# Two transformer layers on one core: 160 planned stretches, lent buffers, a second shift on GpSimd and a lock

## The chip, the cores and the metric

The kernel runs on one core of one Trainium2 chip. The metric is the device time of one execution in microseconds (us), as the median over runs. Five engines work side by side, each on its own list of instructions: TensorE (PE in the profile, its weight loads PEld), VectorE (DVE), ScalarE (ACT), GpSimd (POOL) and SyncE (SP), which issues the transfers.

## The reference

Two layers with shared weights, each attention and then a dense block, over 2048 rows of width 512, 32 heads of width 16, 1792 hidden units, all bfloat16:

```python
def _A_ref(x, wqkv, wo):                       # H = 32, Dh = 16
    qkv = (x @ wqkv).reshape(B, S, 3, H, Dh).transpose(2, 0, 3, 1, 4)
    q, k, v = qkv[0], qkv[1], qkv[2]
    scores = jnp.einsum("bhqd,bhkd->bhqk", q, k) * (Dh ** -0.5)
    o = jnp.einsum("bhqk,bhkd->bhqd", softmax(scores), v)
    return o.transpose(0, 2, 1, 3).reshape(B, S, D) @ wo
def _B_ref(x, w1, b1, w2, b2):
    return gelu(x @ w1 + b1) @ w2 + b2         # tanh form
x = A_x
x = x + _A_ref(layernorm(x), A_wqkv, A_wo)
x = x + _B_ref(layernorm(x), B_w1, B_b1, B_w2, B_b2)
# and both lines once more
```

The exponentials of the softmax are the bulk of the work outside TensorE: 2 layers x 32 heads x 2048 x 2048.

## The kernel before

The work is cut into cells. A cell is the scores of one 128-row tile of keys for 512 columns of padded queries (`QP`, in which a mask on GpSimd, L1192, leaves one of two heads). There are 4096 cells: one matmul each at L1244, on a quarter of the array's rows, so up to four run together. Their results lie in banks of the accumulator memory `ps`; two slots of three banks are filled in turn.

A cell's exponential is taken in one of two ways. ScalarE (L1601) reads a slot of two or three cells and writes `pt`; or VectorE makes it from the bits of a 16-bit integer. That second way has a chain, `dchain`, on a pair of cells in a buffer `du` of four parts: VectorE converts each cell into part 0 (`dfirst`, L1396), GpSimd adds a constant into part 1 (`one`, L1473), and VectorE adds twice that constant to parts 0 and 1, giving 2 and 3 (`two`, L1478). The four parts are then each multiplied with a differently weighted copy of V (`VC`, L1175), so that a VectorE cell needs four matmuls with values where a ScalarE cell needs one. These value products (L1665) run in rounds of four on quarters of the array's columns; a quarter with nothing to do gets a matmul with zeros (L1673).

Only five of the sixteen key tiles of a layer may be VectorE cells (`KD`). Projections, output product and dense block (L556) are the rest of TensorE's work, and fillers (L1232) are matmuls without use, put where TensorE would otherwise stand still too long. GELU runs on ScalarE (L997), which must load another table before and after it.

No order is written out by hand. A planner, run while the program is built, holds a clock for each engine, a list of threads (scores, exponentials, values, projections, layer norms and so on) with priorities, pools of buffers, and a cost for each operation. It always takes the operation that can start first, and writes each engine's instructions in that order, with semaphore waits from the buffers read and written. Constants such as `OPENING`, `TAIL`, `SLACK`, `ALONE`, `PTURG` and `DUURG` steer it. What matters here is that an engine executes its list strictly in the order the planner gave it. Two of its rules are:

```python
        if op.eng == "pool":                   # in _ready: GpSimd behind a VectorE shift
            at = max(t, self.clock["pool"])
            for a, b in self.port_ops[-4:]:
                if a <= at < b - HEAD:
                    at = t = b - HEAD
```

```python
            if self.lend == 2 or s.clock["act"] < s.clock["pe"] + ALONE:   # in chance: a lone VectorE cell
                return self.ended
```

Exponentials use 15 units of `pt`, and at times units lent from memory that is not in use then: two parts of `K` of layer 1, `Q`, and a part of V. `du` has five buffers of its own and one lent late from `K` of layer 0. V of layer 1 shares its memory with partial sums of layer 0 (`PART`); its column of ones is set by one memset when those are done.

Of the kernel before, what the change touches and what calls it, by code (L numbers as in the profile page):

```python
# [13 lines left out]
H = 32  # L14
# [41 lines left out]
QUEUE = 4  # L56
RUSH = 4
# [128 lines left out]
class _Op:  # L186
    __slots__ = ("eng", "cost", "fns", "reads", "writes", "sem", "by", "tail", "prio", "mode", "slack", "late", "back", "port", "limit", "after")

    def __init__(self, eng, cost, fns, reads=(), writes=(), sem=None, by=1, tail=0.0, prio=None, mode="F", slack=None):
# [4 lines left out]
        self.limit = 1e9  # L194
        self.late, self.after = None, []
# [21 lines left out]
class _Sched:  # L217
# [76 lines left out]
    def _ready(self, op):  # L294
# [67 lines left out]
    def run(self):  # L362
        while True:
# [64 lines left out]
            if e == "dve" and op.port:  # L428
                self.port_ops.append((start, start + cost))
# [9 lines left out]
def bass_interleave_layers__mha_block__dense_activation_gelu__prompt_kernel(  # L439
# [15 lines left out]
    with ExitStack() as es:  # L455
# [22 lines left out]
        T["PT"].append(vf[0][:, 0:8192].rearrange("p (n q) -> p n q", q=512))  # L478
# [8 lines left out]
        T["DU"].append(late.rearrange("p (i j q) -> p i j q", i=4, j=2))  # L487
        T["VC"] = sb([128, NKD, 3, H * 17], BF16, "vc")
# [57 lines left out]
class _Plan:  # L546
# [12 lines left out]
    def init(self):  # L559
        T, hbm = self.T, self.hbm  # L560

        def load(dst, src, sem, keys, cost):
# [17 lines left out]
        yield ("need", ("otn", 0, (0, 0, 512), 3))  # L580
        yield _Op("pool", 1.0, lambda e: e.memset(T["V"][1][:, :, :, 16:17], 1.0),
                  writes=["V11"] + ["PART.0.%d" % g for g in range(8)])
        yield ("give", "v1ones")
# [100 lines left out]
    def ln_tile(self, c, t, dst, dkeys, quick):  # L684
# [7 lines left out]
        if not quick:  # L692
            yield _Op("sp", 0.3, lambda e: e.dma_start(dst(t), T["XLN"][:, x, :], transpose=True),
                      reads=["XLN.%d" % x], writes=dkeys(t), sem="dtr%d" % x, by=16, tail=3.5)
            yield ("rel", "xln", x)
            yield ("give", ("lnt", t, ph))
            return
# [14 lines left out]
    def proj(self, l, kind, i, c, src, skeys, ph, done):  # L712
# [44 lines left out]
        if kind == "K":  # L757
            keys = ["K%d.%d.%d" % (l, i, c)]
            if l == 1:
                keys += ["XL.%d" % t for t in range(4 * c, 4 * c + 4)]  # L760
                if c in LEND:
                    yield ("need", ("k1", c))
# [6 lines left out]
        else:  # L769
            yield _Op("dve", DV, lambda e: e.tensor_copy(T["V"][l][:, i, :, 0:16], pb.rearrange("p (h d) -> p h d", h=H)),  # L770
# [166 lines left out]
    def wlate(self, todo):  # L937
        over = ["K0.%d.%d" % (i, c) for i in (0, 1) for c in range(self.NQ)] + ["PART1.%d" % g for g in range(4)]
# [107 lines left out]
    def post(self, l, seg):  # L1046
# [20 lines left out]
        if prev:  # L1067
            yield ("need", ("gfree",) + prev)
        for p in range(NFC // 2):
# [69 lines left out]
    def setup_attention(self):  # L1139
        self.pas = self.passes()  # L1140
        self.alist, self.dlist, self.left, self.pvleft = [], [], [], {}
        self.base, self.span = {}, {}
        n = 0
        for pi, (l, seg, g, kts, part, final) in enumerate(self.pas):
            self.alist.append([(pi, kt, a) for kt in kts if kt not in KD[l] for a in range(4)])
            self.dlist.append([(pi, kt, a) for kt in kts if kt in KD[l] for a in range(4)])
            self.left.append(4 * len(kts))
            n += 4 * len(kts)
# [3 lines left out]
        self.total, self.scored, self.nd, self.pa, self.pv = n, 0, 0, 0, 0  # L1152
        for l in range(NL):
# [4 lines left out]
        self.cap = [2] * (DU // 2) + [1] * (DU % 2) + [2]  # L1158
# [8 lines left out]
    def vcopies(self):  # L1167
        T = self.T
        for l in range(NL):
            yield ("cond", lambda l=l: self.pv >= self.lead[l])  # L1170
            for j, kt in enumerate(KD[l]):
                yield ("need", ("V", l, kt, kt // 4))
                src = T["V"][l][:, kt, :, :].rearrange("p h c -> p (h c)")
                for i, w in enumerate(VW):
                    yield _Op("pool", 0.68, lambda e, j=j, i=i, w=w, src=src: e.tensor_scalar(  # L1175
                        T["VC"][:, j, i, :], src, w, 1.0, op0=ALU.mult, op1=ALU.mult),
                        reads=["V%d.%d" % (l, kt), "V%d1" % l], writes=["VC.%d.%d" % (j, i)])
# [99 lines left out]
    def take(self, c, free):  # L1277
        self.scored += 1
        self.left[c[0]] -= 1
        if self.left[c[0]] == 0:  # L1280
            free.append(self.s.tokens[("qp", c[0])])

    def join(self, op, d, b, extra, free):
# [15 lines left out]
        self.take(d, free)  # L1299
        self.nd += 1  # L1300

    def swap(self, op, start, cells, extra, free, sl):
        if extra or self.lend == 2 or len(cells) < 3 or not (self.open or self.s.pools["du"]):
            return
        if self.s.clock["dve"] > start + SWAP:
            return
# [3 lines left out]
        d = self.next_d({x[2] for x in cells[:-1]}, start)  # L1310
# [8 lines left out]
        if self.left[c[0]] == 1:  # L1319
            free.remove(self.s.tokens[("qp", c[0])])  # L1320
        self.pa = min(self.pa, c[0])
        self.alist[c[0]].insert(0, c)
        self.join(op, d, self.slots[sl][2], extra, free)

    def attach(self, op, start, cells, extra, free):
# [4 lines left out]
        for home in ("dbank", "misc"):  # L1330
            for b in list(pools[home]):
                if len(used) == 4 or self.lend == 2 or not (self.open or pools["du"]):
# [11 lines left out]
                self.join(op, d, b, extra, free)  # L1344

    def scores(self):
        u = 0
        pools = self.s.pools
        while True:
            sl = yield ("acq", "s")  # L1350
            cells = []
            for _ in self.slots[sl]:
# [7 lines left out]
            fns, reads, writes, free, extra = [], [], [], [], []  # L1360
            for c, b in work:
# [7 lines left out]
                self.take(c, free)  # L1369
            ahead = 0.065 + 0.4267 * self.held[1 - sl]  # L1370
            op = _Op("pe", MM, fns, reads=reads, writes=writes, mode="S", slack=max(SLACK, ahead - LATE))
            op.late = lambda op, start, sl=sl, cells=cells, extra=extra, free=free: (self.attach(op, start, cells, extra, free), self.swap(op, start, cells, extra, free, sl))
# [7 lines left out]
            for qs in free:  # L1380
                yield ("rel", "qp", qs)
# [22 lines left out]
    def solo(self):  # L1404
# [10 lines left out]
        while True:  # L1415
# [6 lines left out]
            extra, free = [], []  # L1422
            self.join(op, d, b, extra, free)
# [5 lines left out]
            for qs in free:  # L1429
                yield ("rel", "qp", qs)  # L1430
# [342 lines left out]
```

## Time and profile before

| what | value |
|---|---|
| three timed runs | 1520.94, 1520.66, 1519.98 us |
| median | 1520.66 us |
| profiled execution, span from first to last instruction | 1522.5 us |
| mean granted TensorE clock | 0.997 |
| mean DMA traffic | 68 GB/s |

The profiled execution is given by its span alone; it stands 1.9 us above the median of the timed runs. The busy times of section 1 of the page count an instruction from its start to its end, and ends overlap the next start on ScalarE and VectorE. The groups give, for one kind of instruction, the number, the total busy time, the mean duration, the idle time just before it and what ended that. The chain of waits is followed back from the last instruction. The timeline merges neighbours of one kind and gives the start, the length and the number.

### The profile page before, as it was taken

To read this page: it belongs to the slowest core of one execution; us is meant where nothing else is said; L and a number is where in the kernel's file an instruction comes from. 1 tells how busy PE (TensorE), PEld (TensorE's weight loads), DVE (VectorE), ACT (ScalarE), POOL (GpSimd) and SP (SyncE) were. 2 spreads that over 40 slices of the span, in tenths; PEclk is the share of its full clock that TensorE was granted. 3 is DMA by queue.
4 is the path that set the end of the run, shared out by engine and by line. 5 is a ranking of instruction groups with operands and counts; after the bars stand their busy time and mean duration, and the time that the engine had idled before them with its cause. 6 is when DMAs were issued, how large, how long until landed. Compare 5 with 4: busy or idle time off the path is not lost.

```text
span 1522.5 us, 46554 instructions
## 1 busy us (share of the span) xinstructions
PE 1449.7 (95%) x20337; PEld 446.0 (29%) x20337; DVE 1333.5 (88%) x2255; ACT 1477.5 (97%) x1374; POOL 823.6 (54%) x783
## 2 busy tenths in 40 slices
PE   8998889999999999999999999899999999999998
PEld 2222222222222222222222222222222222344445
DVE  6568888989999899889989889899989999999994
ACT  7999999999999999999999999999999999999995
POOL 5425545556465554646565466556556656564550
PEclk9999999999999999999999999999999999999999
DMA  5200001144121531125221351001143115412522
GB/s 150 47 2 2 2 2 43 29 126 119 29 57 37 153 92 42 37 62 165 62 57 29 91 141 56 15 2 36 43 139 99 36 29 151 124 37 69 157 68 78
DMA packets 145046, 103.40 MB, mean 68 GB/s; under 512 B 37069, under 2 KB 143822, under 8 KB 144846
## 3 DMA queue, kind: packets, MB, share of 16 engines
q1 hardware_dynamic: 144846, 100.44, 23.4%
q8 instruction: 162, 2.65, 0.7%
q14 instruction: 38, 0.31, 0.1%
HBM read 88.61 MB, written 4.19 MB: 61 GB/s over the span
## 4 chain that ended last, share of the span: by engine, by line
ACT 58%; PE 29%; DVE 10%; issue 1%; POOL 1%; DMA 0%; ACTq 0%; DVEq 0%
ACT pt L1601 47%; PE ps L556 10%; PE ps L1244 9%; PE ps L1665 9%; ACT kt L1601 4%; DVE du L1396 4%; ACT g L997 3%; ACT v L1601 2%; DVE du L1478 2%; ACT q L1601 1%; DVE kt L1396 1%; PE ps L1232 1%; DVE g L976 1%; ACT L1601 1%; ACT L997 1%
## 5 line engine op out<-in xcount | busy, mean ns | idle before, releaser
L1601 ACT ACTIVATE pt<-ps 128x1024 bf16<-128x1024 f32 (+1 forms) x1115 | 1195.5, 1213 | 13.5 <-PE ps L1244 9.2
L1473 POOL TENSOR_SCALAR du<-du 128x1024 uint16<-128x1024 uint16 x478 | 558.6, 1170 | 482.9 <-DVE du L1396 469.3
L1396 DVE TENSOR_SCALAR du<-ps 128x512 uint16<-128x512 f32 x955 | 635.6, 683 | 82.5 <-PE ps L1244 77.6
L1244 PE MATMUL ps<-qp,kt 32*128 32x512 bf16 x4096 | 532.0, 385 | 29.9 <-ACT pt L1601 18.1
L1665 PE MATMUL ps<-pt,v 128*17 128x512 bf16 (+1 forms) x2866 | 400.6, 361 | 11.5 <-ACT pt L1601 7.9
L1665 PE MATMUL ps<-du,vc 128*17 128x512 bf16 (+1 forms) x3213 | 372.9, 359 | 5.0 <-DVE du L1478 2.0
L1478 DVE TENSOR_SCALAR du<-du 128x2048 uint16<-128x2048 uint16 x478 | 350.5, 744 | 12.0 <-POOL du L1473 11.7
L1244 PEld LDWEIGHTS ps<-qp,kt 32*128 32x128 bf16 x4096 | 137.7, 91 | 570.0 <-ACT pt L1601 191.9
L1665 PE MATMUL ps<-du,v 128*17 128x512 bf16 (+1 forms) x1071 | 178.9, 360 | 8.0 <-ACT pt L1601 2.2
L1673 PE MATMUL ps<-vc,zero 128*17 128x512 bf16 x805 | 167.0, 381 | 0.0
L556 PE MATMUL ps<-xf,wr 128*32 128x512 bf16 (+1 forms) x1888 | 129.9, 366 | 2.6 <-DMA xf<-xln 1.3
L1665 PEld LDWEIGHTS ps<-pt,v 128*17 128x17 bf16 x2866 | 98.8, 88 | 108.7 <-issue 64.8
L1665 PEld LDWEIGHTS ps<-du,vc 128*17 128x17 bf16 x3213 | 102.3, 89 | 87.7 <-issue 46.0
L556 PE MATMUL ps<-wr,g 128*32 128x512 bf16 x1600 | 117.4, 382 | 1.9 <-DVE du L1396 1.4
L1192 POOL TENSOR_SCALAR qp<-q,mask 128x512 bf16<-128x512 bf16 (+1 forms) x91 | 76.1, 837 | 63.6 <-PE ps L1244 56.5
L1601 ACT ACTIVATE kt<-ps 128x1536 bf16<-128x1536 f32 (+1 forms) x81 | 102.0, 1268 | 5.0 <-PE ps L1244 3.6
L1473 POOL TENSOR_SCALAR kt<-kt 128x1024 uint16<-128x1024 uint16 x45 | 54.6, 1214 | 75.8 <-DVE kt L1396 74.2
L1601 ACT ACTIVATE v<-ps 128x1024 bf16<-128x1024 f32 (+1 forms) x74 | 85.6, 1187 | 2.7 <-PE ps L1244 1.1
L976 DVE TENSOR_SCALAR g<-ps,hb1t 128x512 bf16<-128x512 f32 (+1 forms) x112 | 79.1, 706 | 7.3 <-PE ps L556 7.2
L1396 DVE TENSOR_SCALAR kt<-ps 128x512 uint16<-128x512 f32 x90 | 61.6, 684 | 14.0 <-PE ps L1244 12.3
L1665 PE MATMUL ps<-kt,v 128*17 128x512 bf16 (+1 forms) x314 | 71.1, 365 | 1.4 <-DVE kt L818 0.6
L1665 PEld LDWEIGHTS ps<-du,v 128*17 128x17 bf16 x1071 | 45.8, 89 | 55.0 <-issue 25.6
(90 smaller groups left out, 1242.9 us busy)
## 6 DMA issues: line engine op xcount, KB each, us to landing
wr<-in_B_w_dram SPq DMA_DIRECT2D x256, 256.0 KB, 2.9
wr<-in_A_wqkv_dram SPq DMA_DIRECT2D x24, 256.0 KB, 3.0
wr<-in_A_wo_dram SPq DMA_DIRECT2D x18, 256.0 KB, 2.9
x<-in_A_x_dram SPq DMA_DIRECT2D x7, 512.0 KB, 4.5
kept<-x SPq DMA_DIRECT2D x4, 512.0 KB, 2.9
x<-kept SPq DMA_DIRECT2D x4, 512.0 KB, 3.9
out_dram<-x SPq DMA_DIRECT2D x16, 128.0 KB, 2.8
g<-in_A_wqkv_dram SPq DMA_DIRECT2D x3, 512.0 KB, 5.9
```

What stands on the lines that cost most here:

```text
L556: return [lambda e, a=a: e.matmul(out[32 * a:32 * a + 32, :], lhsT=lhsT[:, 32 * a:32 * a + 32], rhs=rhs, start=start, stop=stop, tile_posi ...
L976: yield _Op("dve", 0.21 + n / 966, lambda e, fc=fc, pb=pb: e.tensor_scalar(T["G"][:, fc, q], pb, T["HB1T"][:, fc:fc + 1], None, op0=ALU.ad ...
L997: lambda e, g=g: e.activation(out=g, in_=g, func=ACT.Gelu_apprx_tanh), reads=gk, writes=gk, prio=2)
L1192: yield _Op("pool", 0.27 + 0.42 * w / 512, lambda e, s=s, q=q, i=i, t=t, w=w: e.tensor_scalar(T["QP"][:, s, w * i:w * i + w], q, T["MASK"] ...
L1232: fns.append(lambda e, o=o, w=w, a=a, m=m: e.matmul(o, lhsT=w, rhs=rhs, start=start, stop=start, tile_position=(0, m * a)))
L1244: return (lambda e: e.matmul(o, lhsT=lhsT, rhs=rhs, start=True, stop=True, tile_position=(32 * a, 0)), ["K%d.%d.%d" % (l, gb, kt // 4), "Q ...
L1396: yield _Op("dve", 0.682, lambda e: e.tensor_scalar(u, self.bank(b), E_SCALE, E_BIAS, op0=ALU.mult, op1=ALU.add), reads=["B.%d" % b], writ ...
L1473: one = _Op("pool", 0.15 + 0.45 * n, lambda e, a=a, b=b: e.tensor_scalar(b, a, float(SHIFT), 1.0, op0=ALU.add, op1=ALU.mult), reads=key[0] ...
L1478: two = _Op("dve", 0.152 + 0.266 * n, lambda e: e.tensor_scalar(U[:, 2:4, 0:n, :], U[:, 0:2, 0:n, :], 2 * SHIFT, None, op0=ALU.add), reads ...
L1601: yield _Op("act", 0.065 + 0.4267 * n, lambda e, src=src, dst=dst: e.activation(out=dst, in_=src, func=ACT.Exp, scale=0.25), reads=["B.%d" ...
L1665: op.fns.append(lambda e, o=o, lhsT=q[0][0][m], rhs=q[0][1][:, n * m:n * m + n], a=a, st=st, sp=sp: e.matmul(o, lhsT=lhsT, rhs=rhs, start= ...
L1673: op.fns.append(lambda e, o=self.bank(b)[32 * a:32 * a + 17, :], rhs=rhs, a=a, st=not begun[a], sp=end: e.matmul(o, lhsT=T["ZERO"][:, 0:17 ...
```

## The change

It is large, and most of it is in the planner.

- `turn`: the progress of the scores is cut into 160 stretches; at the start of each, 30 of the planner's constants are set from one of 50 rows. The choice for each stretch is a fixed list, `PIECES`.
- `dchain`: for a pair whose first shift was planned on GpSimd, the second shift can be split. GpSimd makes part 2 (`more`), and VectorE only part 3 (`far`). A condition on the planner's two clocks and on free `du` buffers decides.
- A lock: when the planner would start a GpSimd operation within the first 0.35 us of a VectorE shift, GpSimd waits on a semaphore for that shift's end.
- Lent buffers: four more for `du`, out of `K` of layer 1, the two halves of V of layer 1 and `K` of layer 0; for `pt`, the memory of `G` (dense block) and `XP` (layer-norm output), which are taken back before their own use.
- V's readiness: a value product is only taken into a round when its V tile's projection is done (`("V", l, ...) in tokens`). The ones column of V of layer 1 is set in two halves.
- Lone VectorE cells: `chance` lets a single VectorE cell go to TensorE also when ScalarE's lead is smaller, if TensorE has no side work, by three new limits. `swap` and `attach` get limits on how many cells join a group.
- A query buffer is given back when the last score that reads it is issued, by a count `due`.
- The planner's cost of a transposing transfer goes from 0.3 to 1.25 us, its landing from 3.5 to 3.2 us.

The core of the diff, with the tables cut:

```diff
+ROWS = (
+    (0.5, 0.3, 0.7, 0.2, 9, 18, 10, 2, 6, 1, 1, 2, 2, 5, 1.5, 1.4, 0.4, 2, 3.5, 24, 3, 4, 0.4, 1.0, 0, 1, 2, 3, 1, 2,),
...
+PIECES = (0, 29, 0, 45, 41, 0, 39, 42, 0, 42, 19, 36, 36, 20, 25, 0, 16, 0, 24, 5, 0, 43, 48, 0, 0, 0, 0, 33, 42, 42, 0, 36, 36, 0, 13, 13, 0, 2, 20,
...
+CLOSE = 0.35
+PMORE = 1
+DUMORE = 2
+GSHUT = 3
+TTAIL = 3.2
...
         if op.eng == "pool":
-            at = max(t, self.clock["pool"])
-            for a, b in self.port_ops[-4:]:
-                if a <= at < b - HEAD:
+            at, op.lock = max(t, self.clock["pool"]), None
+            for a, b, ev in self.port_ops[-4:]:
+                if a <= at < min(a + CLOSE, b - HEAD):
+                    at = t = b + LATENCY["dve"]
+                    op.lock = ev
+                elif a <= at < b - HEAD:
                     at = t = b - HEAD
...
+            if e == "pool" and op.lock:
+                self.P.wait(e, *op.lock)
...
-        self.cap = [2] * (DU // 2) + [1] * (DU % 2) + [2]
+        self.cap = [2] * (DU // 2) + [1] * (DU % 2)
+        self.own = len(self.cap)
+        self.cap += [2] * 5
...
+    def turn(self):
+        self.piece += 1
+        globals().update(zip(NAMES, ROWS[PIECES[self.piece]]))
...
-            if self.lend == 2 or s.clock["act"] < s.clock["pe"] + ALONE:
+            if self.lend == 2:
                 return self.ended
+            if s.clock["act"] < s.clock["pe"] + ALONE:
+                side = sum(th.op.cost for th in s.threads if th.op is not None and th.op.eng == "pe" and th.prio >= 10)
+                if side > SIDE or s.clock["act"] < s.clock["pe"] + BACK or s.clock["dve"] > s.clock["pe"] + SOLO:
+                    return self.ended
...
         yield one
-        yield two
+        if one.eng == "pool" and self.s.clock["pool"] <= self.s.clock["dve"] + PMORE and len(self.s.pools["du"]) >= DUMORE:
+            c, d = U[:, 2, 0:n, :].rearrange("p j q -> p (j q)"), U[:, 3, 0:n, :].rearrange("p j q -> p (j q)")
+            far = _Op("dve", 0.151 + 0.134 * n, lambda e: e.tensor_scalar(U[:, 3, 0:n, :], U[:, 1, 0:n, :], 2 * SHIFT, None, op0=ALU.add),
+                      reads=key[1], writes=key[3])
+            more = _Op("pool", 0.15 + 0.45 * n, lambda e, a=a, c=c: e.tensor_scalar(c, a, float(2 * SHIFT), 1.0, op0=ALU.add, op1=ALU.mult),
+                       reads=key[0], writes=key[2])
+            far.port = more.port = True
+            yield more
+            yield far
+        else:
+            yield two
...
-                            if q and self.s.landed(q[0][2]) <= start:
+                            if q and ("V", l, q[0][5], q[0][5] // 4) in self.s.tokens and self.s.landed(q[0][2]) <= start:
```

More of the change, by code (lines that the diff above doesn't have):

```diff
@@ L1068, in post @@
             yield ("need", ("gfree",) + prev)
+        if not last:
+            yield ("need", ("gin", l, seg))
         for p in range(NFC // 2):
@@ L1298, in join, with swap @@
             op.writes.append("B.%d" % b)
-        self.take(d, free)
+        self.take(d)
         self.nd += 1
-    def swap(self, op, start, cells, extra, free, sl):
-        if extra or self.lend == 2 or len(cells) < 3 or not (self.open or self.s.pools["du"]):
+    def swap(self, op, start, cells, extra, sl):
+        if len(extra) >= BOTH or self.lend == 2 or len(cells) < 3 or not (self.open or self.s.pools["du"]):
             return
         if self.s.clock["dve"] > start + SWAP:
+            return
+        if extra and self.s.clock["dve"] > start + SWAP - 0.6:
             return
@@ L1309, in swap @@
             return
-        d = self.next_d({x[2] for x in cells[:-1]}, start)
+        d = self.next_d({x[2] for x in cells[:-1]} | {x[0][2] for x in extra}, start)
         if d is None:
```

169 lines of the change are left out of this document (131 added, 38 removed), and 53 rows, old and new, of tables (PIECES, ROWS).

## The prediction

> **What bounds the kernel now.** I read the engine totals first, then the chain that ended last.
>
> ```profile
> PE 1449.7 (95%) x20337; PEld 446.0 (29%) x20337; DVE 1333.5 (88%) x2255; ACT 1477.5 (97%) x1374; POOL 823.6 (54%) x783
> ACT 58%; PE 29%; DVE 10%; issue 1%; POOL 1%; DMA 0%; ACTq 0%; DVEq 0%
> ```
>
> ScalarE is busy almost throughout and carries most of the chain. TensorE's 95% holds filler matmuls, and DMA does not appear. So the question is how long ScalarE's list is. The groups by form give the counts, and the timeline of ScalarE at the end gives the real price of one exponential, because start to start leaves out the overlap that a mean duration counts twice.
>
> ```profile
> L1601 ACT ACTIVATE pt<-ps 128x1024 bf16<-128x1024 f32 x768 | 745.0, 1071 | 8.0 <-PE ps L1244 7.1
> L1601 ACT ACTIVATE pt<-ps 128x1536 bf16<-128x1536 f32 x347 | 491.6, 1526 | 5.5 <-PE ps L1665 3.1 <-PE ps L1244 2.1
> ...
> 1487.78 1.94 ACT L1601 ACTIVATE pt<-ps 128x1024 bf16<-128x1024 f32 x2
> 1489.58 1.47 ACT L1601 ACTIVATE v<-ps 128x1536 bf16<-128x1536 f32 x1
> 1490.91 2.83 ACT L1601 ACTIVATE pt<-ps 128x1536 bf16<-128x1536 f32 x2
> 1493.57 1.51 ACT L1601 ACTIVATE v<-ps 128x1536 bf16<-128x1536 f32 x1
> 1494.90 1.10 ACT L1601 ACTIVATE pt<-ps 128x1024 bf16<-128x1024 f32 x1
> 1496.02 1.28 ACT L997 ACT_TABLE_LOAD   x1
> ```
>
> A pair of cells costs (1489.58 - 1487.78) / 2 = 0.90 us, three cells 1490.91 - 1489.58 = 1.33 us. With the same instruction writing into kt, v and q, the groups hold 894 pairs and 421 triples, 3051 cells; VectorE's first pass (L1396, 955 + 90) has the other 1045 of 4096. The exponentials take 894 x 0.90 + 421 x 1.33 = 1364.5 us. The span of 1522.5 us splits into 12.8 us before the first exponential (the same view starts it at 12.77), 26.5 us after the last (1496.0), and 1483.2 us between. In these 1483.2 lie the 1364.5, 14 GELUs (43.9 us), 14 table loads of 1.28 (18 us) and some 3 us of copies. About 53 us are gaps, spread thinly. The three timed runs have a median of 1520.66 us, 1.9 below the span of the profiled execution; I sum in the span and take 1.9 off.
>
> TensorE, VectorE and GpSimd:
>
> ```profile
> 206.59 0.39 PE L1665 MATMUL ps<-du,vc 128*17 128x512 bf16 x4
> 206.91 0.40 PE L1244 MATMUL ps<-qp,kt 32*128 32x512 bf16 x4
> 207.23 0.38 PE L1665 MATMUL ps<-kt,v 128*17 128x512 bf16 x1
> ...
> 207.46 0.38 PE L1665 MATMUL ps<-pt,v 128*17 128x512 bf16 x1
> ...
> L1396 DVE TENSOR_SCALAR du<-ps 128x512 uint16<-128x512 f32 x955 | 635.6, 683 | 82.5 <-PE ps L1244 77.6
> L1473 POOL TENSOR_SCALAR du<-du 128x1024 uint16<-128x1024 uint16 x477 | 557.6, 1170 | 482.2 <-DVE du L1396 468.6 <-DVE mv L668 10.8 <-DVE nmr L676 1.3
> L1478 DVE TENSOR_SCALAR du<-du 128x2048 uint16<-128x2048 uint16 x477 | 349.6, 744 | 12.0 <-POOL du L1473 11.7
> ```
>
> A round of four matmuls takes 0.22 us to the next round (207.23 to 207.46; 0.216 over many), a visit to the scores 0.32 in and 0.32 out, so 0.43 more than staying. GpSimd idles mostly because VectorE has not yet delivered.
>
> **The change, part by part.** All counts of the changed program are from its written order of instructions.
>
> *Cells moved off ScalarE* (lone cells, five lent buffers instead of one, other settings by stretch). VectorE takes 1102 cells, 57 more, ScalarE 2994, as 984 pairs and 342 triples (the seven singles that a count by line shows are table loads). That is +90 x 0.90 - 79 x 1.33 = 81.0 - 105.1 = **-24.1 us** on ScalarE. GELUs, table loads and copies stay in number. This lies on the bounding engine and counts whole, unless another engine becomes late.
>
> *TensorE.* 57 more VectorE cells need four weighted-value products instead of one: value matmuls and their zero fills go from 7104 to 7185 at full width and from 1864 to 1900 at half. That is 81/4 x 0.216 + 36/4 x 0.108 = +5.3 us. Visits to the scores rise from 1314 to 1335: 21 x 0.43 = +9.0. Fillers (L1232) fall from 1252 to 900 small matmuls, 313 rounds to 225: -19.0. Sum -4.7. The 14.3 us of new work cost nothing as long as they replace fillers, 67.6 us of time in which TensorE had nothing to do; without that cover they would be paid in full.
>
> *VectorE.* +57 first passes x 0.683 = +38.9; 134 fewer double second shifts x 0.744 = -99.7; 5 more half-size ones; 160 new single shifts of 128x1024 (the `far` step). No group shows those well: the only 128x1024 of L1478 took 0.884, and half of the double one is 0.37. So they cost 59 to 141; I take 0.45, nearer to the half because one instruction may have been held, and get +72. With 5 x 0.884 the sum is +16 (bounds +3 to +85) against 189 us idle. Hidden; in the busiest stretch, 400 to 600 us, VectorE was busy 190 of 200 us, so the upper bound would not be hidden there.
>
> *GpSimd.* 26 more first shifts and 160 second shifts x 1.17, six small ones at about 1: +224 us, 823.6 to about 1047, 70% of a 1500 us span. Hidden as work. Behind its longer queue stand the masked query copies (L1192), layer-norm applies (L689) and output scaling (L844), for which TensorE and VectorE wait.
>
> *The lock.* At 269 places GpSimd waits for a VectorE shift that has just begun, instead of starting against it. One wait lasts at most about one shift, 0.68 us: up to 180 us on GpSimd, which still has 450 idle. In return VectorE is held less. In the trace L1478 has a median of 0.684 and a mean of 0.744, 0.06 x 522 = 31 us of holding, so the gain is 0 to 31 us on an engine with slack; I take nothing. [...]
>
> *V's readiness, earlier release rules, the opened G and XP buffers, the split memset of the ones column (two half memsets for one).* They forbid a value round before its V tile is written and give more room for exponentials. The DMAs stay 405 in number and kind; SP's transposes and weight loads only change places. I bound these with the gaps: 53 us were idle on ScalarE. Fillers fell by 28%; if gaps fell likewise it would be -15, if a different order misfits by as much it would be +15. I take **-4**, because a search over settings favours short gaps but realizes only part of them.
>
> *The tail.* Before, only table load and GELU follow the last exponential on ScalarE. In the changed order nine VectorE bias passes (L976) and their matmuls still stand between. After the last exponential the rows give TensorE 26.7 instead of 22.4 us, VectorE 15.0 instead of 9.1, and ScalarE the same. Bounds 0 to +5.9; I take **+4.3**, since TensorE was busy 22.5 of those 26.5 us before.
>
> Sum: 1522.5 - 24.1 + 4.3 - 4 = 1498.7, less 1.9: **1497 us**.
>
> **The rivals.**
> *TensorE is the real pace.* For: 29% of the chain, and its work and fillers together almost equal ScalarE's time in each stretch. Against: most of its waits are for ScalarE's buffers. If its other idle time stays as it is, only its own -4.7 remain: 1522.5 - 4.7 - 1.9 = 1516 us.
>
> *Slower: the split pairs come late.* In 160 of 554 pairs a second GpSimd shift (1.04 to 1.17 us) now lies between the first pass and the value products. TensorE takes its work in written order; a round that waits for a late `far` holds the next scores, and with them ScalarE. For: VectorE already waited 20 times for L1473, 0.6 us each, and GpSimd gets 269 new waits. Against: the four lent extra buffers let the products stand later. Lateness of 24/160 = 0.15 us a split pair decides; at 0.3 us it is 160 x 0.3 = 48 us, so 1497 + 48 = 1545 us.
>
> *The clock falls.* With fewer fillers TensorE may be granted half clock more often:
>
> ```profile
> 205.00:213.40 8.40, 6.49 (x86) 1.76 (x78) 5.16 (x9) 8.40 (x8) 3.66 (x4) 1.00 0.01 3
> 213.40:216.80 3.40, 3.35 (x32) 0.83 (x32) 2.01 (x4) 2.70 (x2) 1.34 (x2) 0.50 0.00 0
> ```
>
> The clock column is last but two. After 8.4 us with TensorE busy 77% it was 0.50 for 3.4 us, and again for 6.8 us at 247.5. ScalarE lost 0.7 and 3.4 us in them, 0.4 us for each us. It takes 60 us at half clock to lose the 24: 1521 us. Against: TensorE's real work fills more of the time, not less. [...]
>
> **How the numbers follow.** ScalarE's list sets the time, 1484 to 1510: 0.67. TensorE's pace, 1516: 0.16. Split pairs late, 1545: 0.12. Clock, 1521: 0.05. Runs agree within 0.06%, so 0.2% (3 us) is about what can be told from no change. Faster 0.67 + 0.16 = 0.83, same 0.05, slower 0.12. The lower end is the full gap bound with the tail's cost at zero and a little beyond: 1522.5 - 24.1 - 13 - 1.9 = 1484. The upper end takes in the TensorE case and stops short of the clock's and the late pairs': 1520.
>
> **What would show it.** Right: ScalarE's exponentials 984 and 342 at 0.90 and 1.33 between starts, gaps of 40 to 55 us, a tail near 31, GpSimd near 70%, fewer fillers with the clock mean still 0.99. Wrong: ScalarE waiting long for L1244's scores while TensorE waits for VectorE's or GpSimd's shifts (late pairs); L1478 well above 0.744; a clock mean below 0.98; a tail beyond 33.

## The result and the profile after

The changed kernel takes **1505.82 us** (median of four, 1504.69 to 1506.10) against 1520.80 us of the kernel before on the same chip (1519.98 to 1521.17). The ratio is 0.9901, interval 0.9887 to 0.9915: 15.0 us faster, where 23.8 were forecast and 1497 us named; it lies inside the range of 1484 to 1520.

In the changed program the line numbers are shifted. L1787 is the exponential on ScalarE, L1336 the scores, L1851 the value products, L638 the dense and projection matmuls, L1324 the fillers, L1493 VectorE's first pass, L1610 GpSimd's first shift, L1615 the double second shift, L1621 `far` and L1623 `more`.

The head of the page, busy time of each engine and the chain of waits that ended last:

```profile
span 1502.9 us, 46561 instructions
PE 1443.9 (96%) x20102; PEld 440.9 (29%) x20102; DVE 1346.3 (90%) x2343; ACT 1454.3 (97%) x1385; POOL 918.4 (61%) x975
ACT 43%; PE 39%; DVE 16%; issue 1%; DMA 0%; POOL 0%; SPq 0%; ACTq 0%; DVEq 0%
```

ScalarE's busy time fell by 23.2 us and its share stayed at 97%. VectorE rose by 12.8 us (+16 in the sum). GpSimd rose by 95 us to 61%, not by 224 to 70%. The chain has changed its face: ScalarE 58% to 43%, TensorE 29% to 39%, VectorE 10% to 16%. The mean granted clock is 1.000.

The groups by form (columns: line, engine, shapes, count, then busy time and mean ns of one, then the idle time before them and what ended it):

```profile
L1787 ACT ACTIVATE pt<-ps 128x1024 bf16<-128x1024 f32 x863 | 833.0, 1066 | 15.2 <-PE ps L1336 12.0 <-PE ps L1859 1.1 <-PE ps L1851 0.8
L1787 ACT ACTIVATE pt<-ps 128x1536 bf16<-128x1536 f32 x259 | 370.8, 1493 | 1.6 <-PE ps L1859 0.8 <-PE ps L1336 0.4
L1493 DVE TENSOR_SCALAR du<-ps 128x512 uint16<-128x512 f32 x855 | 566.2, 682 | 55.4 <-PE ps L1336 50.6
L1615 DVE TENSOR_SCALAR du<-du 128x2048 uint16<-128x2048 uint16 x308 | 224.0, 743 | 8.6 <-POOL du L1610 8.5
L1621 DVE TENSOR_SCALAR du<-du 128x1024 uint16<-128x1024 uint16 x117 | 57.5, 499 | 0.0
L1610 POOL TENSOR_SCALAR du<-du 128x1024 uint16<-128x1024 uint16 x425 | 443.8, 1048 | 297.1 <-DVE du L1493 159.0 <-DVE du L1615 72.4 <-DVE v L1615 19.6
```

With all destinations the exponentials are 984 pairs and 342 triples, 0.90 and 1.33 us from start to start as before. `far` took 0.50 us, near the 0.45 taken. L1615 kept its mean of 0.743. GpSimd's first shift, though, fell from 1.170 to 1.048 us: that goes with the lock, which turns being held into waiting (without its waits, below, the mean is 1.136). The idle time before L1610 shows it, 72.4 us waiting for L1615 where the page before named no such wait.

ScalarE's timeline at the end (start, length, line, count, and in brackets the idle time before it and what ended it):

```profile
1464.31 2.93 ACT L1787 ACTIVATE pt<-ps 128x1536 bf16<-128x1536 f32 x2
1466.97 4.49 ACT L1787 ACTIVATE v<-ps 128x1536 bf16<-128x1536 f32 x3
1471.48 1.28 ACT L1077 ACT_TABLE_LOAD   x1
1472.77 1.70 ACT L1077 ACTIVATE g<-g 128x1792 bf16<-128x1792 bf16 x1
1477.52 1.70 ACT L1077 ACTIVATE g<-g 128x1792 bf16<-128x1792 bf16 x1 [3.05 <-DVE g L1056]
1484.38 0.59 ACT L784 COPY xf<-ps 128x512 bf16<-128x512 bf16 x1 [5.16 <-PE ps L778]
```

The last exponential ends at 1471.5 and the tail is 31.4 us (before 26.5): +4.9, for which the sum had +4.3. The second half of GELU waits 3.05 us for a bias pass, as the prediction said of those nine passes.

So the profiled execution splits like this, against that of before:

| part | before | after | difference |
|---|---|---|---|
| up to the first exponential | 12.8 | 13.1 | +0.3 |
| exponentials, number x typical time from start to start (0.903 and 1.330) | 1367.2 | 1343.4 | -23.8 |
| the rest between first and last | 116.0 | 115.0 | -1.0 |
| tail | 26.5 | 31.4 | +4.9 |
| span | 1522.5 | 1502.9 | -19.6 |

The rest between holds GELU, table loads and gaps. One gap is new: 7.8 us where layer 0 meets layer 1. The timeline of ScalarE, and then that of TensorE with VectorE's copy, at that place:

```profile
740.58 5.56 ACT L1787 ACTIVATE pt<-ps 128x1536 bf16<-128x1536 f32 x5
753.97 3.77 ACT L1787 ACTIVATE pt<-ps 128x1024 bf16<-128x1024 f32 x4 [7.82 <-PE ps L1336]
```

```profile
749.27 2.55 PE L1324 MATMUL ps<-vc 128*32 128x512 bf16 x44
751.64 1.04 PE L638 MATMUL ps<-xp,wr 128*32 128x512 bf16 x16
752.79 0.68 DVE L834 CAST kt<-ps 128x512 bf16<-128x512 f32 x1
753.53 0.61 PE L1336 MATMUL ps<-qp,kt 32*128 32x512 bf16 x6
```

The scores of L1336 need keys of layer 1, whose projection (L638) runs at 751.64 and whose copy ends at 753.47. Ahead of that projection, from 749.27 on, TensorE has fillers only (44). Before, the longest gap at this place was 0.81 us.

### The profile page after: what moved, and what is told of

Same layout as the page of the kernel before. It is cut to its first block, busy times and chain, and to the rows that moved or that the text cites. A ratio compares the mean times of both kernels' runs of the same rounds, so it can differ in the third digit from the quotient of the medians.

```text
span 1502.9 us, 46561 instructions
## 1 busy us (share of the span) xinstructions
PE 1443.9 (96%) x20102; PEld 440.9 (29%) x20102; DVE 1346.3 (90%) x2343; ACT 1454.3 (97%) x1385; POOL 918.4 (61%) x975
## 4 chain that ended last, share of the span: by engine, by line
ACT 43%; PE 39%; DVE 16%; issue 1%; DMA 0%; POOL 0%; SPq 0%; ACTq 0%; DVEq 0%
ACT pt L1787 34%; PE ps L1851 13%; PE ps L638 13%; PE ps L1336 13%; DVE du L1493 6%; DVE du L1615 3%; ACT g L1077 3%; ACT kt L1787 2%; ACT v L1787 1%; ACT g L1787 1%; DVE kt L1493 1%; DVE v L1493 1%; ACT xp L1787 1%; PE ps L1324 1%; DVE stats L744 1%
## 5 line engine op out<-in xcount | busy, mean ns | idle before, releaser
L1787 ACT ACTIVATE pt<-ps 128x1024 bf16<-128x1024 f32 (+1 forms) x1122 | 1166.3, 1164 | 16.8 <-PE ps L1336 12.5
L1610 POOL TENSOR_SCALAR du<-du 128x1024 uint16<-128x1024 uint16 x430 | 446.9, 1043 | 300.7 <-DVE du L1493 159.0
L1493 DVE TENSOR_SCALAR du<-ps 128x512 uint16<-128x512 f32 x855 | 566.2, 682 | 55.4 <-PE ps L1336 50.6
L1336 PE MATMUL ps<-qp,kt 32*128 32x512 bf16 x4096 | 547.8, 384 | 27.6 <-ACT pt L1787 13.4
L1851 PE MATMUL ps<-pt,v 128*17 128x512 bf16 (+1 forms) x2795 | 384.4, 359 | 6.4 <-ACT pt L1787 1.6
L1851 PE MATMUL ps<-du,vc 128*17 128x512 bf16 (+1 forms) x2883 | 347.4, 357 | 2.5 <-DVE du L1615 1.6
L1336 PEld LDWEIGHTS ps<-qp,kt 32*128 32x128 bf16 x4096 | 140.9, 91 | 577.3 <-ACT pt L1787 172.4
L1615 DVE TENSOR_SCALAR du<-du 128x2048 uint16<-128x2048 uint16 (+1 forms) x313 | 226.1, 738 | 9.4 <-POOL du L1610 9.2
L1851 PE MATMUL ps<-du,v 128*17 128x512 bf16 (+1 forms) x961 | 159.2, 359 | 5.1 <-DVE du L1615 1.2
L638 PE MATMUL ps<-xf,wr 128*32 128x512 bf16 (+1 forms) x1888 | 128.8, 365 | 1.0 <-DVE g L1056 0.9
L1623 POOL TENSOR_SCALAR du<-du 128x1024 uint16<-128x1024 uint16 x117 | 122.7, 1049 | 8.1 <-DVE du L1621 5.1
L1851 PEld LDWEIGHTS ps<-pt,v 128*17 128x17 bf16 x2795 | 93.6, 88 | 101.8 <-issue 63.9
L1493 DVE TENSOR_SCALAR kt<-ps 128x512 uint16<-128x512 f32 x167 | 113.6, 682 | 8.8 <-PE ps L1336 6.1
L638 PE MATMUL ps<-wr,g 128*32 128x512 bf16 x1600 | 119.8, 383 | 1.5 <-DVE du L1493 0.5
L1610 POOL TENSOR_SCALAR kt<-kt 128x1024 uint16<-128x1024 uint16 x84 | 87.7, 1045 | 52.4 <-DVE du L1615 25.6
L1851 PEld LDWEIGHTS ps<-du,vc 128*17 128x17 bf16 x2883 | 94.2, 89 | 74.8 <-issue 45.0
L1851 PE MATMUL ps<-kt,vc 128*17 128x512 bf16 (+1 forms) x621 | 103.2, 339 | 0.1
L1787 ACT ACTIVATE kt<-ps 128x1024 bf16<-128x1024 f32 (+1 forms) x77 | 94.4, 1242 | 1.1 <-PE ps L1336 0.3
L1851 PE MATMUL ps<-kt,v 128*17 128x512 bf16 (+1 forms) x393 | 92.2, 360 | 1.4 <-DVE v L909 0.4
```

Source lines behind the costliest of these rows:

```text
L638: return [lambda e, a=a: e.matmul(out[32 * a:32 * a + 32, :], lhsT=lhsT[:, 32 * a:32 * a + 32], rhs=rhs, start=start, stop=stop, tile_posi ...
L1336: return (lambda e: e.matmul(o, lhsT=lhsT, rhs=rhs, start=True, stop=True, tile_position=(32 * a, 0)), ["K%d.%d.%d" % (l, gb, kt // 4), "Q ...
L1493: yield _Op("dve", 0.682, lambda e: e.tensor_scalar(u, self.bank(b), E_SCALE, E_BIAS, op0=ALU.mult, op1=ALU.add), reads=["B.%d" % b], writ ...
L1610: one = _Op("pool", 0.15 + 0.45 * n, lambda e, a=a, b=b: e.tensor_scalar(b, a, float(SHIFT), 1.0, op0=ALU.add, op1=ALU.mult), reads=key[0] ...
L1615: two = _Op("dve", 0.152 + 0.266 * n, lambda e: e.tensor_scalar(U[:, 2:4, 0:n, :], U[:, 0:2, 0:n, :], 2 * SHIFT, None, op0=ALU.add), reads ...
L1623: more = _Op("pool", 0.15 + 0.45 * n, lambda e, a=a, c=c: e.tensor_scalar(c, a, float(2 * SHIFT), 1.0, op0=ALU.add, op1=ALU.mult), reads=k ...
```

## The experiments

Two theories stood against each other. **ScalarE's list is the bound**: what leaves it, leaves the time, and the other engines have slack. **The four engines are interlocked**: each keeps its written order, buffers tie them together, so that relief on one is used up by waits for the next. Two further questions were the lock and the order picked by stretch. The runs come from several chips; taken as ratios to the kernel before on the same chip, the differences below change by less than 1 us.

**Relief on ScalarE alone.** The order stays exactly as written; 82 exponentials read and write one cell of their two or three, 44 us less by the start-to-start prices. The left-out cells are missing from the result.

```diff
             dst = self.unit(run)
+            if u >= 150 and u % 11 == 0 and run[-1] < PT_RING:
+                src, dst = self.bank(self.slots[sl][0], 1).rearrange("p (j q) -> p j q", j=1), self.unit(run[:1])
```

> The changed kernel with its order untouched, but 82 of ScalarE's exponentials take only the first of their two or three cells (the other cells of those tiles keep old values, so part of the softmax is left out). That relieves ScalarE by 60 x 0.427 + 22 x 0.853 = 44 us. If ScalarE's list alone sets the time: 1505.8 - 44 = 1462 us, give or take 4. If TensorE paces together with it (rival): less than half comes through, 1490 or more. If late pairs on VectorE and GpSimd pace: nothing comes through, 1503 or more.

Measured 1501.51 us, ratio 0.9877 (0.9861 to 0.9893): 4.3 us of 44. That is in the branch of TensorE pacing together with ScalarE, at its weak end. The two executions at a granted clock of 1.000 took 1499.7 us, 6.1 less than the changed kernel; those at 0.998 and 0.999 took 1504.9 and 1503.3. The chain of waits in this run, and ScalarE's waits (in total, times, longest):

```profile
PE 54%; DVE 25%; ACT 18%; issue 1%; DMA 1%; POOL 0%; DVEq 0%; ACTq 0%
ACT pt L1789 <- PE ps L1336: 35.8, 84, 7.8
```

The chain has gone over to TensorE. In the changed kernel the second row reads 12.5 us in 14 waits. What ScalarE saves it then spends waiting for scores; the rest is spread thinly.

**Relief on TensorE alone.** Of the dense block's products 768 matmuls, 192 rounds, are left out of TensorE's list, and so their share of the sums; 192 x 0.216 = 41 us.

```diff
-                fns += self.quads(pb, T["G"][:, 2 * p + j, q], ws[j], p + j == 0, False)
+                four = self.quads(pb, T["G"][:, 2 * p + j, q], ws[j], p + j == 0, False)
+                for f in four:
+                    f.drop = p > 0 and j == 0
+                fns += four
...
         s.run()
+        self.P.prog["pe"] = [x for x in self.P.prog["pe"] if x[0] == "wait" or not getattr(x[1], "drop", False)]
```

> The changed kernel with its order untouched, but 192 rounds of four matmuls of the dense block's second product are left out (12 of its 28 half-pieces of every tile row except the first pair), which relieves TensorE by 192 x 0.216 = 41 us, spread over the whole span. If ScalarE's list alone sets the time: 1500 to 1506, only holes such as the 7.8 us at the layer change and the tail can shrink. If TensorE paces: 1465 to 1485.

Measured 1502.17 us, ratio 0.9879 (0.9864 to 0.9894): 3.7 us of 41. Taken alone this agrees with a lone bound on ScalarE as well (1500 to 1506 expected); only together with the relief on ScalarE does it speak for interlocking. TensorE's longest row of waits is still that for ScalarE, and twice as long:

```profile
PE ps L1339 <- ACT pt L1790: 26.1, 84, 1.6
```

In the changed kernel the same wait stands at 13.4 us in 35.

**Relief on VectorE alone, and on GpSimd alone.** 143 first passes convert 256 of 512 columns; 69 first shifts on GpSimd treat half of their columns. The other halves keep old values. The reliefs of 143 x 0.267 = 38 us and 69 x 0.43 = 29 us are estimates: in the trace of before VectorE's bias passes (L976) take 0.658 us from start to start at 512 columns and 0.391 at 256, and in the changed kernel GpSimd's first shift takes 1.043 us (median) at 128x1024 and 0.617 at 128x512. In the runs VectorE's busy time fell by 26.1 us and GpSimd's by 35.2.

```diff
+        self.firsts += 1
+        m = 256 if self.firsts > 100 and self.firsts % 7 == 0 else 512
-        u = self.T["DU"][pair["du"]][:, 0, j, :]
+        u = self.T["DU"][pair["du"]][:, 0, j, 0:m]
...
```

```diff
+            self.shifts += 1
+            m = 256 * n if self.shifts > 50 and self.shifts % 6 == 0 else 512 * n
...
-e.tensor_scalar(b, a, float(SHIFT), ...
+e.tensor_scalar(b[:, 0:m], a[:, 0:m], float(SHIFT), ...
```

> The changed kernel with its order untouched, but 143 of VectorE's first passes convert only half of their 512 columns (the rest keeps old values), which relieves VectorE by 143 x 0.267 = 38 us. ScalarE theory and TensorE theory alike: no change within 3 us, 1503 to 1507. If VectorE with the added shifts paces, as the late-pairs rival has it: 1475 to 1495.

> The changed kernel with its order untouched, but 69 of GpSimd's first shifts work on half of their columns (the rest keeps old values), which relieves GpSimd by 69 x 0.43 = 29 us and brings those pairs 0.43 us earlier. ScalarE theory and TensorE theory alike: no change within 3 us, 1503 to 1507. Late pairs: 1480 to 1498.

Measured 1504.27 us (ratio 0.9896, 0.9880 to 0.9913) and 1503.85 us (0.9889, 0.9874 to 0.9904): 1.5 of 38 and 2.0 of 29 us, each too close to the changed kernel's own interval to be told from it with certainty. Both lie where a pace set by ScalarE or by TensorE had put them (1503 to 1507), far from the range for late pairs.

**Relief on ScalarE and TensorE together.** Both edits of above at once.

> The changed kernel with its order untouched, and both reliefs at once: the 82 shortened exponentials (44 us) and the 192 rounds of the dense block left out (41 us). If ScalarE and TensorE hold each other, and nobody else: where both are relieved the time falls, though their places do not coincide, so 10 to 25 us below the 1505.8, that is 1481 to 1496. If VectorE, GpSimd or the fixed order hold as well: 1496 to 1501, little more than the 3 to 4 us of each alone.

Measured 1494.12 us, ratio 0.9819 (0.9802 to 0.9837): 11.7 us of 85. That is more than 4.3 + 3.7, but the intervals of the three runs are too wide to tell 11.7 from 8.0. The expected range for VectorE, GpSimd or the fixed order holding as well, 1496 to 1501, was missed; the time lies in the other, ScalarE and TensorE holding each other (1481 to 1496), near its upper end. The chain of waits in the run:

```profile
PE 42%; ACT 29%; DVE 27%; issue 1%; POOL 0%; DMA 0%; POOLq 0%; DVEq 0%; ACTq 0%
```

VectorE now has 27% of the chain where it had 16%, as it would if a third engine comes forward when two are relieved. So ScalarE and TensorE hold each other, and some 73 of the 85 us are still held by something else; whether by VectorE or by the fixed order alone is not separated.

**The same reliefs on the kernel before**, one at a time: 88 exponentials cut (47 us), and the same 192 rounds left out (41 us).

> The kernel before with its order untouched, but 88 of ScalarE's exponentials take only their first cell (the others keep old values): 65 x 0.427 + 23 x 0.853 = 47 us less for ScalarE. After the changed kernel gave only some 4 us for 44, two theories: the kernel before had a lone bound, ScalarE, and the change has used it up: 1520.6 - 35 to 47 = 1474 to 1485 us. Or both orders are interlocked alike, TensorE's list being written to fit ScalarE's: 1512 to 1519.

> The kernel before with its order untouched, but the same 192 rounds of the dense block's second product left out, 41 us less for TensorE. A lone bound on ScalarE: no change, 1518 to 1521. Interlocked orders: 2 to 5 us less, 1515 to 1519, as the changed kernel gave.

Measured 1516.21 us with less ScalarE work (ratio 0.9968, 0.9955 to 0.9981; 4.6 us less) and 1519.95 us with less TensorE work (0.9993, 0.9983 to 1.0003). So ScalarE was no lone bound before either, although it had 58% of the chain. At a clock of 1.000 this run took 1513.6 and 1513.8 us, 7.1 less; at 0.998 its other four took 1516.0 to 1517.1. The median of the second run lies where a lone bound on ScalarE was expected (1518 to 1521), not in the interlocked range (1515 to 1519), and it holds a surprise: its ten executions spread from 1516.67 to 1522.3 us and follow the granted clock, from 0.998 to 0.992, where the kernel before shows 0.999 to 1.000. In the trace of before the clock was 0.50 for 3.4 and 6.8 us, and its mean 0.997. With stretches at 0.50 here too, the mean falls by half of their share, so 0.006 more is by estimate 2 x 0.006 x 1520 = 18 us at half clock, for 5.6 us of time: about 0.3 us lost per us. At 0.998 the relief is 4.1 us, like the others. In the relief on ScalarE after the change the same estimate gives 5.2 us for about 6 us between 1.000 and 0.998, so the price is not one number.

**The lock.** The order stays as written; only the 269 waits of GpSimd for a VectorE shift that has just begun are not issued.

```diff
-            if e == "pool" and op.lock:
-                self.P.wait(e, *op.lock)
```

> The changed kernel with its order untouched, but the 269 waits of the lock are not written (the order was planned as if they were there). If the lock costs GpSimd time that counts: 1500 to 1504 us. If GpSimd's and VectorE's holding each other matters and the lock spares it: 1508 to 1515, with the mean of VectorE's shifts above 0.743. If both are hidden, as the prediction took it: 1504 to 1507, and only the holding shows, in the mean durations.

Measured **1548.47 us**, ratio 1.0184 (1.0170 to 1.0197): 43 us more than the changed kernel, and slower than the kernel before. None of the three expected ranges, 1500 to 1515 in all, holds it. The head of its page:

```profile
span 1549.3 us, 46532 instructions
PE 1457.2 (94%) x20102; PEld 440.4 (28%) x20102; DVE 1396.0 (90%) x2343; ACT 1466.7 (95%) x1385; POOL 999.6 (65%) x975
PE 40%; DVE 40%; ACT 17%; issue 2%; DMA 0%; POOL 0%; DVEq 0%; ACTq 0%
```

Its groups by form:

```profile
L1613 DVE TENSOR_SCALAR du<-du 128x2048 uint16<-128x2048 uint16 x308 | 248.5, 822 | 2.0 <-POOL du L1608 1.8
L1619 DVE TENSOR_SCALAR du<-du 128x1024 uint16<-128x1024 uint16 x117 | 70.5, 609 | 0.0
L1608 POOL TENSOR_SCALAR du<-du 128x1024 uint16<-128x1024 uint16 x425 | 481.4, 1136 | 308.2 <-DVE du L1491 299.7 <-DVE mv L744 4.2 <-DVE nmr L752 3.2
```

Same instructions, same order (the lines stand two lower): VectorE's busy time is 49.7 us longer, its double shift 0.822 instead of 0.743 us, `far` 0.609 instead of 0.499, and GpSimd's first shift 1.136 instead of 1.048. VectorE takes 40% of the chain instead of 16%. So 49.7 us more on VectorE (and 81.2 more on GpSimd, which the chain names with 0%) went with 43 us more at the end, while 38 us less on VectorE gave 1.5. The lower clock of these runs, 0.994 to 0.998, does not explain it: the execution at 0.998 still took 1547.7 us.

The traces also tell which engine is held when. A GpSimd shift of 128x1024 that started while a second shift of VectorE (L1615 or L1621) was running took over 0.1 us more than its median of 1.043 us in every case: 178 of 178 before (1.39 to 1.52 us), 14 of 14 in the changed kernel, 183 of 183 here. Of those that started outside one, 2 of 344, 2 of 694 and 13 of 525 did. VectorE's second shift took over 0.1 us more than its own median only when a GpSimd operation was already running at its start (88 of 143 before, 88 of 187 after, 155 of 239 here), and never otherwise (0 of 380, 367 and 315). So the waits spare GpSimd directly. VectorE's mean of 0.743 us against a median of 0.685 in the changed kernel is as before: they do not free VectorE of holding, and only keep it from growing in this order.

A plan made without the lock was not run; so 43 us is the price of leaving the waits out of an order that counts on them, and not what the lock gained over the kernel before.

**The order picked by stretch.** Everything else of the change stays; all 160 stretches use the first row, and the planner makes its own order from it.

```diff
-PIECES = (0, 29, 0, 45, 41, 0, 39, 42, 0, 42, 19, 36, 36, 20, 25, 0, 16, 0, 24, 5, 0, 43, 48, ...
+PIECES = (0,)
```

> The changed kernel with the first row of settings in all 160 stretches: every part of the change but the choice by stretch; its order is planned anew. Counted from its written order it has 932 pairs and 382 triples on ScalarE, 3010 cells: 932 x 0.903 + 382 x 1.330 = 1349.7 against 1367.2 before, 17 us less. If a shorter list of ScalarE is the gain whatever the order: 1520.7 - 17 + some 5 for a longer tail = 1506 to 1512 us. If the lists hold each other and the choice by stretch is what turns 57 moved cells into time: 1516 to 1523, nothing gained.

Measured 1518.32 us, ratio 0.9983 (0.9974 to 0.9992): 2.3 us faster than before on the same chip, in the range for lists that hold each other (1516 to 1523). Yet its exponentials are 932 pairs and 382 triples, 1349.7 us from start to start, 17.5 less than before. In its profiled execution the tail is 33.1 us and the rest between first and last exponential 119.3 us (before 116.0, of which some 3.5 were half clock). Most of the shorter list is thus gone again before any pick: as tail, as other time between, and as half clock that the profiled execution of before had and this one has not. Between this run and the changed kernel lie 12.0 us of span: 6.3 of list, 4.3 of the rest between, 1.7 of tail, less 0.3 at the start.

**The split of the second shift undone.** Meant to leave the order as it was: `far` makes both parts, and `more` only 32 columns that are then overwritten. The changed operands changed what the planner saw, so it made another order (1076 VectorE cells, 949 pairs, 374 triples, 131 split pairs), and the premise of the expectation does not hold.

```diff
-U[:, 3, 0:n, :], U[:, 1, 0:n, :], ...  reads=key[1], writes=key[3])
+U[:, 2:4, 0:n, :], U[:, 0:2, 0:n, :], ...  reads=key[0] + key[1], writes=key[2] + key[3])
...
-e.tensor_scalar(c, a, float(2 * SHIFT), ...
+e.tensor_scalar(c[:, 0:32], a[:, 0:32], float(2 * SHIFT), ...
```

> The changed kernel with its order untouched, but in the 160 split pairs VectorE makes both last parts in one pass (0.60 instead of 0.335 start to start, +42 us for VectorE), and GpSimd's second shift touches only 32 columns (some 0.9 us less each, -145 us for GpSimd). Late pairs, where GpSimd's second shift delays the products: faster, 1495 to 1503. If the split spares VectorE time that counts: slower, 1508 to 1520. If both are hidden: 1504 to 1507.

Measured 1545.41 us, ratio 1.0162 (1.0148 to 1.0176). It does not price the split by itself. Its `far` (96 in `du`, 0.750 us) ran for what the planner costed at 0.42. It is 40 us slower than the changed kernel, with VectorE at 29% of the chain; that fits what unplanned VectorE time did above, but how much of it belongs to the other order is not known.

**The gap at the layer change.** Seven weighted copies of V stand on GpSimd just ahead of the layer-norm apply that the late projection needs:

```profile
741.53 4.98 POOL L1267 TENSOR_SCALAR vc<-v 128x544 bf16<-128x544 bf16 x7 [0.36 <-DVE ott L923]
746.61 1.52 POOL L767 TENSOR_SCALAR xln<-x,rstd,nmr 128x512 bf16<-128x512 bf16 x2
```

The first experiment gives the copies a later priority (8 instead of 4).

```diff
-        s.spawn(self.vcopies(), 4)
+        s.spawn(self.vcopies(), 8)
```

> The changed kernel, only with the weighted copies of V (L1267) planned behind the layer norms instead of ahead of them, so that at the layer change the second pair of layer-norm applies does not wait on GpSimd behind seven copies of 0.72 us. The order changes from there on; the exponentials stay 984 and 342. Theory: those copies are a part of the 7.8 us hole in ScalarE at 746 us; up to 5 us come back, 1501 to 1504. Rival: the hole is set by TensorE's dense work being late, then nothing, 1505 to 1507.

Measured 1504.84 us, ratio 0.9896 (0.9880 to 0.9911). The timeline of ScalarE at that place:

```profile
752.33 6.69 ACT L1787 ACTIVATE pt<-ps 128x1024 bf16<-128x1024 f32 x7 [6.61 <-PE ps L1336]
```

The gap shrinks from 7.8 to 6.6 us, so the copies are 1.2 us of it; the time falls by 1.0, which the intervals do not tell from nothing. In the changed kernel the last of the four transposes ahead of the projection was issued at 748.6 and landed 2.5 us later, 0.5 us before the projection; with the copies later it landed at 748.6, 1.3 us before. What holds the rest is open.

**Other picks.** On top of that, 13 of the 160 choices changed, ten of them in the last stretches.

> The kernel with the copies later, and 13 of the 160 stretches given another of the 50 rows, 12 of them among the last 20, so that the dense work of the last but one part no longer piles up behind the last exponential. Counted from its written order, ScalarE still has 984 pairs and 342 triples. If the longer tail (31.4 us in the changed kernel, 26.5 before) is a cost of the picks and not of the moved cells: the tail falls to 25 to 27 and the time to 1497 to 1501 us. If what is won at the end is given back as gaps in the last stretches: 1502 to 1505.

Measured 1503.10 us, ratio 0.9880 (0.9863 to 0.9896), the lowest median of the versions that compute everything, 2.7 us below the changed kernel; the intervals of the two overlap. ScalarE's timeline at the end:

```profile
1474.80 1.54 ACT L1783 ACTIVATE pt<-ps 128x1536 bf16<-128x1536 f32 x1
1476.36 1.28 ACT L1073 ACT_TABLE_LOAD   x1
1477.65 3.28 ACT L1073 ACTIVATE g<-g 128x1792 bf16<-128x1792 bf16 x2
1485.87 0.59 ACT L780 COPY xf<-ps 128x512 bf16<-128x512 bf16 x1 [4.93 <-PE ps L774]
```

The two GELU halves now run without a wait, and the tail is 1503.1 - 1476.3 = 26.8 us, 4.6 less. The stretch from first to last exponential is 1460.5 us, 2.1 more. The tail's cost came from the picks and can be had back, with nearly half given back as gaps, and the time is in the range of that branch (1502 to 1505). The span of this execution, the slowest of the four, does not show the gain (1503.1 against 1502.9): its first exponential starts at 15.8 us instead of 13.1, ahead of any pick that differs.

## Why the prediction was right and wrong

**The sign and the main term.** 24.1 us on ScalarE's list were forecast, and with the counts and the time from start to start of the trace it is 23.8. That is little of a test, because the counts were read from the written order.

The step that failed is the next one, "this lies on the bounding engine and counts whole": the reliefs show 4.3 us of 44 after and 4.6 of 47 before (6 to 7 at a clock of 1.000), and with one row, 17.5 us of shorter list brought 2.3. Between that run and the changed kernel only the choice by stretch differs, and it brings 12.5 us; the likely reason is that the picked order moved the other lists along with ScalarE's. What the lent buffers, the split or V's readiness add was not separated.

The chain's 58% for ScalarE was read as a bound; it was one thread of an interlocked schedule, and the condition "unless another engine becomes late" was the normal state. The time thus lies in the branch "ScalarE's list sets the time" without that branch's reason, which is luck in part. The lower end of the range was added up with 13 us of gaps where the text's own bound is 15.

**Where the missing 9.0 us lie** (the sum unrounded is 1496.8). The step from span to median failed first: the sum took 1.9 us off because the profiled execution of before lay above the timed median. In every listed run the time is the span *plus* 1.8 us; the profiled execution simply lay about 3.5 us above the other executions, most of which had spans of 1518.3 to 1519.5 at a clock of 0.999 to 1.000 where it had 0.997. The half clock at 213.4 and 247.5 us, seen and quoted, belonged in this step. The step makes 3.7 us, and the profiled execution of after lay 1.1 below its median, for no reason that the runs show. The second failed term is "I take -4" for gaps: the rest between fell by 1.0 (3.0 off), and without the half clock of before it rose by an estimated 2.5, for which the 7.8 us at the layer change are more than enough. Tail, list and start make the last 1.2: 3.7 + 1.1 + 3.0 + 1.2 = 9.0.

**The lock: "I take nothing".** Against the kernel before, VectorE won nothing by it: its double shift has a mean of 0.743 us as against 0.744. But the reason, an engine with slack, was wrong. The mean of 0.744 against a median of 0.684 measured the holding of before's order; nothing in that trace showed what an order with 160 more shifts on GpSimd would suffer, so the bound "0 to 31" was that of another program. In the changed order the waits are worth 43 us, more than the whole gain. With the waits left out VectorE's busy time rises by 49.7 us to 1396.0, still 153 us below the span, and the time by 43 us. Busy time below the span was no slack.

**GpSimd +224, measured +95.** The count was right and the price not: with the lock the first shift takes 1.048 us and the second 1.05, not 1.17, and the time appears as waiting. That is some 85 of the missing 129 us; masked copies, layer norms and output scaling became 25 us shorter in the same way. It stayed hidden as work.

**VectorE and TensorE.** VectorE +16 forecast, +12.8 measured, `far` 0.45 and 0.50. TensorE's busy time fell by 5.8 us, -4.7 in the sum.

**The tail.** +4.3 forecast, +4.9 measured, with the mechanism as told.

**The rivals.** *TensorE is the pace* named 1516 us, which did not come, but its row of the chain rose to 39%, and relief on TensorE is worth as much as on ScalarE. It was right that ScalarE is not alone and wrong that TensorE would be. *Split pairs late*: VectorE waited for GpSimd's first shift 13 times, 9.2 us (before 20 times, 11.7), far from 0.15 us a split pair; and TensorE's value products and their weight loads waited 3.6 us in all for `far` and `more`. It did not happen. *The clock falls*: not in the changed kernel; its price came out at 0.3 to 0.9 us per us in the reliefs, against 0.4. The case that did end slower was one that the prediction did not list: the same order without the lock's waits.

## What to carry to other kernels

In a kernel whose engines run fixed orders through shared buffers, ScalarE at 97% and the largest share of the chain do not make a lone bound: shorten one engine's list in the unchanged order, and see how much of it reaches the end (here a tenth to a seventh), before counting it whole. Such a run prices the fixed order only; a plan made anew can do better or worse. Time added to this tight order passed almost in full (43 us at the end for 49.7 on VectorE), so the protections against contention are terms of the sum even where the engine has idle time. Take the step from span to time from several executions, and look for half clock in the profiled one first.

## What the runs showed of the hardware

Where GpSimd started a 128x1024 shift during a second shift of VectorE, the shift took over 0.1 us more than its median (375 of 375 in three traces; 1.39 to 1.52 us instead of 1.04 in the trace of before). VectorE's second shift took over 0.1 us more than its median in over half of the cases in which a GpSimd operation was running at its start (331 of 569), and in none of the 1062 others. VectorE's first passes, which read the accumulator memory, kept 0.68 us in all three traces. Without the 269 waits VectorE's busy time is 49.7 us longer and GpSimd's 81.2 us; with them GpSimd's first shift takes 1.048 us and GpSimd waits instead (72.4 us before L1610 for L1615), while VectorE's double shift keeps its mean of before (0.743 us against a median of 0.685). In the kernel before, 192 rounds left out of TensorE's list lowered the granted clock (0.999 to 1.000 down to 0.992 to 0.998), and at the median that took back most of the 4.1 us which the relief gave at 0.998. In the two runs with less work on ScalarE some executions had 0.998 too, and were 2.3 to 5.2 us slower than those at 1.000.
